# One-bank PSUM accumulators in the MLP, w1 loads spread over the last attention stage, layernorm transposes in the third step of a cycle

## The chip, the core and the metric

The kernel runs on one core of a Trainium2 chip. Five engines work side by side, each through its own list of instructions in order: TensorE (PE; its weight loads appear as PEld), VectorE (DVE), ScalarE (ACT), GpSimd (POOL) and SyncE (SP), which here only issues transfers. They wait for each other through semaphores. Matmul results go to PSUM, 8 banks of 128 partitions x 2 KB; a matmul of 512 float32 columns fills one bank. The metric is device time in microseconds; lower is better. The span in a trace reaches from the first to the last instruction.

## The reference

A transformer block on 2048 tokens of width 1024, all in bfloat16: attention with 32 heads of 32 and a causal window of 256 tokens, then an MLP of width 3584, each behind a layernorm without parameters and with a residual.

```python
def _A_ref(x, wqkv, wo):
    H = 32; Dh = D // H; W = 256
    qkv = (x @ wqkv).reshape(B, S, 3, H, Dh).transpose(2, 0, 3, 1, 4)
    q, k, v = qkv[0], qkv[1], qkv[2]
    scores = einsum("bhqd,bhkd->bhqk", q, k) * (Dh ** -0.5)
    mask = (idx[:, None] - idx[None, :] >= 0) & (idx[:, None] - idx[None, :] < W)
    p = softmax(where(mask, scores, -1e9))
    o = einsum("bhqk,bhkd->bhqd", p, v)
    return o.transpose(0, 2, 1, 3).reshape(B, S, D) @ wo
def _B_ref(x, w1, w2):
    return einsum("bsf,fd->bsd", silu(einsum("bsd,df->bsf", x, w1)), w2)
h  = A_x + _A_ref(layernorm(A_x), A_wqkv, A_wo)
h2 = h + _B_ref(layernorm(h), B_w1, B_w2)
```

## The kernel before

The 2048 tokens are worked in four blocks of 512 (`b`), each of four tiles of 128 (`j`). The order of the instructions is the order in which the code is written; nothing reorders it. Each engine takes its instructions in that order, and SP's transfers are issued in that order too.

The stages follow each other:

1. *Projection of block 0*: for each of four tiles a layernorm (`ln_stats`, `ln_rstd`, `ln_norm`), its transposes on PE and the v projection; then 16 groups for q and k (`qk_group`), with the layernorm of block 1 between them.
2. *Three attention stages* (`b` = 1, 2, 3): attention of block b-1, mixed with the projections of block b. A stage has 24 steps `n`, three for each of eight groups of four heads. A step computes the scores of one of three kinds of key pieces, `A`, `B`, `C` (PE), their exponentials (ACT) and masks (POOL), one projection group of eight matmuls (`dense[n]`, DVE casts it out), one piece of the tail of the head group before (`pending`), and perhaps one step of the next block's layernorm (`steps`). The tail has three pieces: in the first and second step of a cycle `attn_out` (attention times v into the tile `o_ps`, reciprocal and product on DVE), in the third `attn_transpose` (four transposes into the tile `tp_ps`, a DVE copy out).
3. *The last attention stage*: attention of block 3, where the 24 projection groups are the output projections of blocks 0 to 2 (`wo_group`). DVE adds the residual, a tile of `t_in` that SP loads (`load_res`), and the sum goes to `h_dram`. From step 9 on it also does the layernorm of block 0 for the MLP (`ln2_steps`), which begins with a load of h from `h_dram` (L316).
4. *The MLP*, block after block: 28 groups of the first product (`h1_group`, L402), each followed by `silu`, a tanh on ACT (L411) and a product on DVE (L412) that both read the accumulator; then eight groups of 28 matmuls of the second product (L444) with a residual add on DVE (L446) and a store, and the layernorm of the next block between them. The first block also takes in the rest of the attention tail and the output projection of block 3.

*Accumulators.* `next_acc` goes round the list `acc_banks`. Up to the MLP that is the two tiles `acc0` and `acc1` of one bank each. In the MLP four more banks join: the scores' tiles `sc0` and `sc1`, two banks each, of which each half is one accumulator (L397). The framework puts a wait ahead of an instruction that touches a tile which others still read or write.

```python
sc = [ps.tile([P, 2, 512], F32, name=f"sc{i}") for i in range(2)]            # L81
tp_ps = ps.tile([P, 1024], BF16, name="tp_ps")                               # L83
acc_banks += [sc[i][:, j, :] for i in range(2) for j in range(2)]            # L397
```

*Transposes.* A layernorm tile takes eight PE transposes into `tp_ps` (L173), which they fill, and one DVE copy out (L174). `attn_transpose` uses the same tile (L282, L283). In attention stages 1 and 2 a layernorm step is taken from step 4 on in the first two steps of each cycle: four of statistics, one reciprocal root (`ln_rstd`, L159 to L165, four Newton iterations of three instructions), four normalizations and four transposes, the last in steps 18, 19, 21 and 22.

*Loads.* All transfers are issued by SP. The eight w1 loads (L363, 896 KB each) come at once after the third attention stage, ahead of the first residual loads of the last one. w2 comes in seven pieces of 1 MB: piece 0 in step 9 of the last stage just ahead of the h load, the others in the MLP. `t_in` and `t_out` lie in the region `r_t`, which also holds the transposed layernorm of the odd blocks.

Of the kernel before, what the change touches and what calls it, by code (L numbers as in the profile page):

```python
# [14 lines left out]
P = 128  # L15
# [21 lines left out]
def kernel(  # L37
# [43 lines left out]
    sc = [ps.tile([P, 2, 512], F32, name=f"sc{i}") for i in range(2)]  # L81
# [72 lines left out]
    def ln_rstd(st, rs, lo, hi):  # L154
        n = hi - lo
        var = small.tile([P, 4], F32, name="ln_var", tag="ln_var")
        t = small.tile([P, 4], F32, name="ln_t", tag="ln_t")
        va, ta, y = var[:, 0:n], t[:, 0:n], rs[:, lo:hi]
        nc.vector.tensor_scalar(out=va, in0=st[:, lo:hi, 1], scalar1=LN_EPS, scalar2=None, op0=ALU.add)  # L159
        nc.vector.tensor_scalar(out=y.bitcast(I32), in0=va.bitcast(I32), scalar1=1, scalar2=None, op0=ALU.logical_shift_right)  # L160
        nc.vector.tensor_scalar(out=y.bitcast(I32), in0=y.bitcast(I32), scalar1=-1, scalar2=0x5F3759DF, op0=ALU.mult, op1=ALU.add)
        for _ in range(4):
            nc.vector.scalar_tensor_tensor(out=ta, in0=y, scalar=-0.5, in1=va, op0=ALU.mult, op1=ALU.mult)
            nc.vector.tensor_tensor(out=ta, in0=ta, in1=y, op=ALU.mult)
            nc.vector.scalar_tensor_tensor(out=y, in0=ta, scalar=1.5, in1=y, op0=ALU.add, op1=ALU.mult)  # L165
# [136 lines left out]
    def ln1_steps(b):  # L302
# [6 lines left out]
        for j in range(4):  # L309
            steps.append(lambda j=j: ln_transpose(xs[j], lnT_b[b % 2], j, dve))  # L310
        return steps
# [14 lines left out]
    steps = ln1_steps(1)  # L326
# [9 lines left out]
    for b in range(1, NB):  # L336
        dense = [lambda j=j, c=c: v_group(b, j, c, dve) for j in range(4) for c in range(2)]
        dense += [lambda w=w, g=g: qk_group(b, w, g, dve) for g in range(G) for w in range(2)]
        if b + 1 < NB:
            for j in range(4):  # L340
                load_x(b + 1, j)
            steps = ln1_steps(b + 1)
        else:
            steps = []
# [3 lines left out]
        for g in range(G):  # L348
            for kind in KINDS:
# [4 lines left out]
                if steps and n >= 4 and n % 3 != 2:  # L354
                    steps.pop(0)()
                n += 1
            pending = tail_of(b - 1, g)
        while steps:
            steps.pop(0)()


    for kt in range(KT):
        nc.sync.dma_start(out=w1[:, kt, :], in_=w1_v[:, kt, :])  # L363
# [7 lines left out]
    n = 0  # L371
    for g in range(G):
        for kind in KINDS:
# [7 lines left out]
            if pending:  # L381
                pending.pop(0)()
            if n == 9:
                steps = ln2_steps(0)
                nc.sync.dma_start(out=w2[0], in_=w2_v[:, 0:4, :])
# [11 lines left out]
    acc_banks += [sc[i][:, j, :] for i in range(2) for j in range(2)]  # L397
# [18 lines left out]
    for b in range(NB):  # L416
# [4 lines left out]
        for ft in range(FT):  # L421
# [7 lines left out]
            if b == 0 and 6 <= ft < 14:  # L429
# [3 lines left out]
                wo_group(NB - 1, j, c)  # L433
        if b == 0:
            load_w2(6)
        steps = ln2_steps(b + 1) if b + 1 < NB else []
        load_res(b, 0, h_dram)
# [47 lines left out]
```

## Time and profile before

| | us |
|---|---|
| median of 3 runs | 846.25 (846.16 to 846.5) |
| the profiled execution, its own time | 846.29 |
| its span | 844.6 |
| PE busy | 724.2 |
| PE weight loads busy (beside PE) | 353.4 |
| DVE busy | 329.5 |
| ACT busy | 257.1 |
| POOL busy | 171.6 |

Mean granted TensorE clock: 0.98 of full speed. DMA is 16.9% busy with the kernel's own queue.

How to read it: a busy time is the sum of an engine's instructions over the span. Engines work at the same time, so the times don't add up; the engine with the largest share sets the pace only where it is not itself waiting. The view of waits gives the idle time of an engine ahead of an instruction, by what ended it. The timeline shows instructions in order of time, neighbours of one kind merged (x16 is 16 of them), with the idle time ahead of the first one and its releaser in brackets. A few matmul records are missing, so x15 can stand for 16.

### The profile page before, as it was taken

How to read it: one execution, taken by the hardware profiler on the slowest of the kernel's cores; microseconds unless marked ns; L12 is line 12 of the kernel's file. 1: busy time of each engine (PE TensorE's matmuls, PEld its weight loads, DVE VectorE, ACT ScalarE, POOL GpSimd, SP SyncE). 2: the span in 40 equal slices, each digit the busy share in tenths (PEclk: the TensorE clock that was granted, in tenths of full speed). 3: DMA queues.
4: the chain of work that ended last, by engine and by line, in shares of the span. 5: the costliest groups of instructions: out<-in, count | busy, mean ns of one | idle time of the engine just before them, and what ended most of it. 6: DMA issues, size and time to landing. Idle time of an engine off the chain costs nothing.

```text
span 844.6 us, 12753 instructions
## 1 busy us (share of the span) xinstructions
PE 724.2 (86%) x5265; PEld 353.4 (42%) x5358; DVE 329.5 (39%) x738; ACT 257.1 (30%) x325; POOL 171.6 (20%) x375
## 2 busy tenths in 40 slices
PE   6999999999992978888779877789887889878898
PEld 2445555555551544433334433334333334333443
DVE  7446756754440456433324223223232242232111
ACT  3226557667771655311200022200022200122100
POOL 1006556666761645200000000000000000000000
PEclk9999999999996989999999999999999999999999
DMA  9310010010008242541041000021100020100010
GB/s 318 130 50 2 2 51 2 2 43 11 2 19 356 101 163 89 177 153 45 1 134 41 19 31 1 1 75 32 44 0 1 0 81 32 38 0 1 6 44 26
DMA packets 28138, 49.06 MB, mean 58 GB/s; under 512 B 1968, under 2 KB 12208, under 8 KB 28080
## 3 DMA queue, kind: packets, MB, share of 16 engines
q1 hardware_dynamic: 28080, 48.24, 16.9%
q8 instruction: 42, 0.69, 0.3%
q14 instruction: 16, 0.13, 0.0%
HBM read 39.85 MB, written 8.39 MB: 57 GB/s over the span
## 4 chain that ended last, share of the span: by engine, by line
PE 77%; DVE 10%; DMA 8%; ACT 3%; issue 2%; SPq 0%; ACTq 0%; DVEq 0%
PE sc L402 15%; PE sc L444 13%; PE acc L201 12%; PE acc L444 8%; PE acc L402 7%; PE acc L193 7%; PE acc L211 4%; PE o_ps L265 4%; PE sc L229 3%; DMA r_t<-in_A_x_dram 3%; DVE r_a L412 3%; DMA r_e<-h_dram 2%; ACT r_a L411 2%; DVE r_t L446 2%; PE tp_ps L173 1%
## 5 line engine op out<-in xcount | busy, mean ns | idle before, releaser
L240 ACT ACTIVATE r_e<-sc 128x1024 bf16<-128x1024 f32 (+2 forms) x192 | 175.8, 967 | 112.7 <-PE sc L229 112.7
L255 POOL TENSOR_SCALAR_AFFINE_SELECT r_e<-r_e 128x256 bf16<-128x256 bf16 (+1 forms) x368 | 168.6, 487 | 176.4 <-ACT r_e L240 172.5
L402 PEld LDWEIGHTS <-r_w 128*128 128x128 bf16 x896 | 87.1, 97 | 166.3 <-issue 65.0
L402 PE MATMUL sc<-r_e,r_w 128*128 128x512 bf16 x452 | 105.0, 379 | 41.4 <-DVE r_a L412 38.8
L444 PEld LDWEIGHTS <-r_a 128*128 128x128 bf16 x896 | 88.1, 99 | 121.9 <-issue 20.5
L444 PE MATMUL sc<-r_a 128*128 128x512 bf16 x548 | 125.9, 386 | 13.9 <-DVE r_t L446 13.3
L411 ACT ACTIVATE r_n<-sc 128x512 f32<-128x512 f32 x30 | 17.9, 597 | 252.4 <-PE sc L402 249.7
L444 PE MATMUL acc<-r_a 128*128 128x512 bf16 x327 | 73.7, 379 | 1.0 <-DMA r_a<-in_B_w_dram 0.6
L201 PEld LDWEIGHTS <-r_w 128*128 128x128 bf16 x512 | 46.1, 98 | 59.4 <-issue 10.3
L203 DVE CAST r_a<-acc 128x512 bf16<-128x512 f32 x56 | 38.5, 688 | 69.9 <-PE acc L201 69.7
L265 PE MATMUL o_ps<-r_a,r_e 128*128 128x33 bf16 x1440 | 46.4, 178 | 18.6 <-DVE r_n L273 18.6
L201 PE MATMUL acc<-r_t,r_w 128*128 128x512 bf16 x240 | 58.0, 380 | 3.0 <-issue 1.7
L265 PEld LDWEIGHTS <-r_e 128*128 128x128 bf16 x1440 | 45.9, 96 | 34.3 <-issue 19.7
L201 PE MATMUL acc<-r_w 128*128 128x512 bf16 x244 | 57.0, 379 | 1.7 <-issue 0.9
L211 PE MATMUL acc<-r_o,r_a 128*128 128x512 bf16 x195 | 51.5, 404 | 5.9 <-DVE r_t L213 4.3
L412 DVE SCALAR_TENSOR_TENSOR r_a<-r_n,sc 128x512 bf16<-128x512 f32 x30 | 20.6, 688 | 78.3 <-ACT r_n L411 78.3
L402 PE MATMUL acc<-r_e,r_w 128*128 128x512 bf16 x208 | 48.6, 379 | 0.4
L402 PE MATMUL sc<-r_a,r_w 128*128 128x512 bf16 x139 | 33.4, 378 | 13.7 <-DVE r_a L412 8.6
L446 DVE SCALAR_TENSOR_TENSOR r_t<-sc,r_t 128x512 bf16<-128x512 f32 x20 | 13.7, 684 | 77.1 <-PE sc L444 77.1
L229 PE MATMUL sc<-r_a 32*128 32x128 bf16 (+2 forms) x704 | 40.5, 279 | 0.0
L211 PEld LDWEIGHTS <-r_a 128*128 128x128 bf16 x256 | 24.0, 101 | 36.9 <-issue 14.2
L213 DVE TENSOR_TENSOR r_t<-acc,r_t 128x512 bf16<-128x512 f32 x26 | 17.8, 685 | 45.1 <-PE acc L211 25.3
(69 smaller groups left out, 509.7 us busy)
## 6 DMA issues: line engine op xcount, KB each, us to landing
r_w<-in_B_w_dram SPq DMA_DIRECT2D x8, 896.0 KB, 11.9
r_a<-in_B_w_dram SPq DMA_DIRECT2D x7, 1024.0 KB, 9.5
r_w<-in_A_wqkv_dram SPq DMA_DIRECT2D x6, 1024.0 KB, 11.2
r_o<-in_A_x_dram SPq DMA_DIRECT2D x16, 256.0 KB, 7.7
r_t<-in_A_x_dram SPq DMA_DIRECT2D x16, 256.0 KB, 2.8
h_dram<-r_t SPq DMA_DIRECT2D x16, 256.0 KB, 2.0
r_t<-h_dram SPq DMA_DIRECT2D x16, 256.0 KB, 2.8
out_dram<-r_t SPq DMA_DIRECT2D x32, 128.0 KB, 1.7
```

The lines of the kernel that those rows point to most:

```text
L193: nc.tensor.matmul(acc, lhsT=lnT_b[b % 2][:, kt, j * P:(j + 1) * P], rhs=wqkv[:, kt, col0:col0 + 512], start=(kt == 0), stop=(kt == KT - 1))
L201: nc.tensor.matmul(acc, lhsT=wqkv[:, kt, col0:col0 + P], rhs=lnT_b[b % 2][:, kt, :], start=(kt == 0), stop=(kt == KT - 1))
L203: copy(out=(qT, kT)[which][b][:, g, :], in_=acc)
L211: nc.tensor.matmul(acc, lhsT=qT[b][:, g, j * P:(j + 1) * P], rhs=wo[:, g, c * 512:(c + 1) * 512], start=(g == 0), stop=(g == G - 1))
L229: nc.tensor.matmul(sc[hh // 2][:, hh % 2, ch * P:(ch + nq) * P], lhsT=kT[t // 4][r0:r0 + DH, g, (t % 4) * P:(t % 4 + 1) * P], rhs=qT[b][r0 ...
L240: nc.scalar.activation(out=e[:, :, lo:hi], in_=sc[pair][:, :, lo:hi], func=ACT.Exp, scale=scale)
L255: nc.gpsimd.affine_select(out=ap, in_=ap, pattern=[[0, 2], [0, n], [sgn, P]], compare_op=ALU.is_ge if upper else ALU.is_gt, fill=0.0, base ...
L265: nc.tensor.matmul(o_ps[:, qt * 2 + hh, 0:VW], lhsT=e_of(i, kind, pair)[:, hh, ch * P:(ch + 1) * P], rhs=v[:, b * 4 + kt, g * 4 + pair * 2 ...
L402: nc.tensor.matmul(acc, lhsT=w1[:, kt, ft * P:(ft + 1) * P], rhs=ln2T[b][:, kt, :], start=(kt == 0), stop=(kt == KT - 1))
L411: nc.scalar.activation(out=th, in_=acc, func=ACT.Tanh, scale=0.5)
L412: nc.vector.scalar_tensor_tensor(out=gT[:, ft, :], in0=th, scalar=1.0, in1=acc, op0=ALU.add, op1=ALU.mult)
L444: nc.tensor.matmul(acc, lhsT=gT[:, ft, j * P:(j + 1) * P], rhs=w2[ft // 4][:, ft % 4, c * 512:(c + 1) * 512], start=(ft == 0), stop=(ft == ...
```

## The change

Five edits, in the order of the program.

- The scores' tiles `sc0`, `sc1` move to a pool of their own, which is closed ahead of the MLP. A new pool takes its place with four tiles of one bank each, `hacc0` to `hacc3`, and these join `acc_banks`.
- `ln_rstd` does three Newton iterations, not four.
- In attention stages 1 and 2 the layernorm steps start at step 1 (step 3 is left out), nine of them up to step 10; the four transposes are a list of their own, `turns`, taken in steps 11, 14, 17 and 20, the third steps of their cycles. The layernorm of block 1 keeps its order.
- The w1 loads are issued one by one in the even steps 0 to 14 of the last stage; w2's piece 0 moves from step 9 to step 17.
- In the MLP the first residual load of a block (`load_res(b, 0, h_dram)`) is issued ahead of w2's last piece.

```diff
@@ -78,7 +78,9 @@
-    sc = [ps.tile([P, 2, 512], F32, name=f"sc{i}") for i in range(2)]
+    ps_sc = tc.tile_pool(name="ps_sc", bufs=1, space=bass.MemoryType.PSUM, reuse_waits="tile")
+    sc_pool = ps_sc.__enter__()
+    sc = [sc_pool.tile([P, 2, 512], F32, name=f"sc{i}") for i in range(2)]
@@ -159,7 +161,7 @@
-        for _ in range(4):
+        for _ in range(3):
@@ -306,9 +308,7 @@
-        for j in range(4):
-            steps.append(lambda j=j: ln_transpose(xs[j], lnT_b[b % 2], j, dve))
-        return steps
+        return steps, [lambda j=j: ln_transpose(xs[j], lnT_b[b % 2], j, dve) for j in range(4)]
@@ -323,7 +323,7 @@
-    steps = ln1_steps(1)
+    steps = sum(ln1_steps(1), [])
@@ -339,9 +339,9 @@
-            steps = ln1_steps(b + 1)
+            steps, turns = ln1_steps(b + 1)
         else:
-            steps = []
+            steps, turns = [], []
@@ -351,16 +351,15 @@
-                if steps and n >= 4 and n % 3 != 2:
+                if steps and n >= 1 and n != 3:
                     steps.pop(0)()
+                elif turns and n % 3 == 2:
+                    turns.pop(0)()
                 n += 1
             pending = tail_of(b - 1, g)
-        while steps:
-            steps.pop(0)()
-
-
-    for kt in range(KT):
-        nc.sync.dma_start(out=w1[:, kt, :], in_=w1_v[:, kt, :])
+        assert not steps and not turns
@@ -380,8 +379,11 @@
+            if n % 2 == 0 and n // 2 < KT:
+                nc.sync.dma_start(out=w1[:, n // 2, :], in_=w1_v[:, n // 2, :])
             if n == 9:
                 steps = ln2_steps(0)
+            if n == 17:
                 nc.sync.dma_start(out=w2[0], in_=w2_v[:, 0:4, :])
@@ -394,7 +396,9 @@
-    acc_banks += [sc[i][:, j, :] for i in range(2) for j in range(2)]
+    ps_sc.__exit__(None, None, None)
+    ps_h1 = ctx.enter_context(tc.tile_pool(name="ps_h1", bufs=1, space=bass.MemoryType.PSUM, reuse_waits="tile"))
+    acc_banks += [ps_h1.tile([P, 512], F32, name=f"hacc{i}")[:] for i in range(4)]
@@ -431,10 +435,10 @@
+        load_res(b, 0, h_dram)
         if b == 0:
             load_w2(6)
         steps = ln2_steps(b + 1) if b + 1 < NB else []
-        load_res(b, 0, h_dram)
```

The line numbers of the changed kernel are others: L402 becomes L406, L444 becomes L448, L206 L208, L216 L218, L363 L383, L173 L175, L174 L176, L203 L205, L282 to L283 L284 to L285.

*PE in the first MLP product*, where one group ends and the next begins in the same two-bank tile; `sc_78` is `sc0`, `r_w` holds w1, `r_a` the transposed layernorm of block 0. Before:

```order
L402 MATMUL sc_78<-r_a,r_w 128x512
L402 LDWEIGHTS r_w
L402 MATMUL sc_78<-r_a,r_w 128x512 [waits DVE_49]
L402 LDWEIGHTS r_w
L402 MATMUL sc_78<-r_a,r_w 128x512
```

and at the same place now:

```order
L406 MATMUL hacc_4649<-r_a,r_w 128x512
L406 LDWEIGHTS r_w
L406 MATMUL hacc_4650<-r_a,r_w 128x512 [waits DVE_49]
L406 LDWEIGHTS r_w
L406 MATMUL hacc_4650<-r_a,r_w 128x512
```

The two groups write two tiles now, and each group has a wait of its own for DVE, also those on `acc` and on the first halves, which had none.

*DVE in attention stage 1*, around the first layernorm transpose. L203 casts a projection group out, L272 and L273 belong to `attn_out`, L283 copies the attention transposes out of `tp_ps`, L174 a layernorm tile. Before:

```order
L203 CAST r_a<-acc_82 128x512 [waits PE_49]
L283 COPY r_a<-tp_ps 128x512 [waits PE_49,Activation_49]
L203 CAST r_a<-acc_83 128x512 [waits PE_49]
L272 RECIPROCAL recip<-o_ps 128x8 [waits PE_49]
L273 TENSOR_TENSOR r_n<-o_ps,recip 128x4x64 [waits DVE_49]
L174 COPY r_w<-tp_ps 128x8x128 [waits PE_49]
```

and around the first one now:

```order
L205 CAST r_a<-acc_86 128x512 [waits PE_49]
L285 COPY r_a<-tp_ps 128x512 [waits PE_49,Activation_49]
L176 COPY r_w<-tp_ps 128x8x128 [waits PE_49]
L205 CAST r_a<-acc_85 128x512 [waits PE_49]
L274 RECIPROCAL recip<-o_ps 128x8 [waits PE_49]
L275 TENSOR_TENSOR r_n<-o_ps,recip 128x4x64 [waits DVE_49]
```

The layernorm copy has moved from behind `attn_out` to directly behind the copy of the attention transposes.

*SP at the begin of the last attention stage.* `r_w<-in_B_w_dram` is a w1 load, `r_t<-in_A_x_dram` a residual load, `h_dram<-r_t` a store of h; waits on DMAHW are for earlier transfers. Before, with six more w1 loads ahead:

```order
L363 DMA r_w<-in_B_w_dram 128x3584 [waits DMAHW6_49,PE_49]
L363 DMA r_w<-in_B_w_dram 128x3584 [waits DMAHW7_49]
L206 DMA r_t<-in_A_x_dram 128x1024 [waits DMAHW0_49,DVE_49]
L206 DMA r_t<-in_A_x_dram 128x1024 [waits DMAHW1_49]
L216 DMA h_dram<-r_t 128x1024 [waits DMAHW2_49,DVE_49]
L206 DMA r_t<-in_A_x_dram 128x1024 [waits DMAHW3_49,DMAHW0_49]
```

and now:

```order
L346 DMA r_o<-in_A_wo_dram 128x4x1024 [waits DMAHW7_49,DVE_49,PE_49]
L208 DMA r_t<-in_A_x_dram 128x1024 [waits DMAHW0_49,DVE_49,PE_49]
L208 DMA r_t<-in_A_x_dram 128x1024 [waits DMAHW1_49,PE_49]
L383 DMA r_w<-in_B_w_dram 128x3584 [waits DMAHW2_49]
L218 DMA h_dram<-r_t 128x1024 [waits DMAHW3_49,DVE_49]
L208 DMA r_t<-in_A_x_dram 128x1024 [waits DMAHW4_49,DMAHW0_49]
L383 DMA r_w<-in_B_w_dram 128x3584 [waits DMAHW5_49]
```

The residual loads stand ahead of w1 now, and one w1 load stands behind each further one.

## Rows read from the trace of the kernel before

**Rows 1.** The page: engines' busy us (share) xinstructions; granted clock in 40 slices.

```profile
PE 724.2 (86%) x5265; PEld 353.4 (42%) x5358; DVE 329.5 (39%) x738; ACT 257.1 (30%) x325; POOL 171.6 (20%) x375
...
PEclk9999999999996989999999999999999999999999
```

**Rows 2.** Waits of PE: engine line waited for, us in total, times, longest us.

```profile
PE sc L402 <- DVE r_a L412: 47.4, 33, 1.5
PE o_ps L265 <- DVE r_n L273: 18.6, 2, 16.6
PE sc L444 <- DVE r_t L446: 13.3, 8, 3.2
...
PE sc L402 <- DVE r_t L213: 4.9, 6, 1.0
...
PE acc L211 <- DVE r_t L213: 4.3, 1, 4.3
...
PE sc L402 <- DVE r_t L446: 2.4, 3, 0.8
```

**Rows 3.** Timeline, first MLP product of block 1: start us, us, engine, line.

```profile
498.57 0.69 DVE L412 SCALAR_TENSOR_TENSOR r_a<-r_a,sc 128x512 bf16<-128x512 f32 x1 [1.04 <-ACT r_a L411]
499.31 3.61 PE L402 MATMUL sc<-r_e,r_w 128*128 128x512 bf16 x16 [1.41 <-DVE r_a L412]
...
504.39 1.89 PE L402 MATMUL sc<-r_e,r_w 128*128 128x512 bf16 x8 [1.47 <-DVE r_a L412]
...
512.86 3.61 PE L402 MATMUL sc<-r_e,r_w 128*128 128x512 bf16 x16 [1.41 <-DVE r_a L412]
```

**Rows 4.** Timeline, PE: q and k groups of block 0; second MLP product.

```profile
29.52 17.43 PE L201 MATMUL acc<-r_w 128*128 128x512 bf16 x79
...
563.82 13.93 PE L444 MATMUL sc<-r_a 128*128 128x512 bf16 x55 [3.07 <-DVE r_t L446]
...
685.74 12.25 PE L444 MATMUL sc<-r_a 128*128 128x512 bf16 x55 [3.11 <-DVE r_t L446]
```

**Rows 5.** Timeline, PE: cycle starts ahead of the last attention stage; stops in it.

```profile
236.51 0.51 PE L229 MATMUL sc<-r_a 32*128 32x384 bf16 x8
...
244.53 0.51 PE L229 MATMUL sc<-r_a 32*128 32x384 bf16 x8
...
274.26 0.85 PE L265 MATMUL o_ps<-r_a,r_e 128*128 128x33 bf16 x24 [16.62 <-DVE r_n L273]
...
310.21 0.59 PE L211 MATMUL acc<-r_o,r_a 128*128 128x512 bf16 x1 [4.26 <-DVE r_t L213]
...
324.14 0.75 PE L265 MATMUL o_ps<-r_a,r_e 128*128 128x33 bf16 x24 [1.95 <-DVE r_n L273]
...
338.15 0.61 PE L173 MATMUL tp_ps<-ident,r_a 128*128 128x128 bf16 x8 [0.89 <-DVE r_a L283]
...
347.40 1.89 PE L402 MATMUL acc<-r_a,r_w 128*128 128x512 bf16 x8
```

**Rows 6.** Timeline, SP and DVE: the first residual loads of the last stage.

```profile
256.97 2.46 SPq L206 DMA_DIRECT2D r_t<-in_A_x_dram  x2
...
272.95 0.69 DVE L213 TENSOR_TENSOR r_t<-acc,r_t 128x512 bf16<-128x512 f32 x1 [19.50 <-DMA r_t<-in_A_x_dram]
```

**Rows 7.** DMA issues: transfers xcount, KB each, median us to landing.

```profile
r_t<-in_A_x_dram SPq DMA_DIRECT2D x16, 256.0 KB, 2.8
...
r_e<-h_dram SPq DMA_DIRECT2D x3, 1024.0 KB, 5.8
...
r_a<-h_dram SPq DMA_DIRECT2D x1, 1024.0 KB, 9.2
```

**Rows 8.** PE behind the root in stages 1, 2; one root instruction: us, mean ns.

```profile
93.11 1.89 PE L201 MATMUL acc<-r_t,r_w 128*128 128x512 bf16 x7 [1.00 <-DVE r_a L203]
...
157.74 1.89 PE L201 MATMUL acc<-r_w 128*128 128x512 bf16 x7 [0.47 <-DVE r_a L203]
...
L163 DVE SCALAR_TENSOR_TENSOR ln_t<-rs_a,ln_var 128x1 f32<-128x1 f32 x16 | 2.5, 159 | 0.6
```

## The prediction

> **What bounds the kernel now.** I read the busy times first, then what TensorE (PE) waited for, then PE's timeline stage by stage. PE is busy 724.2 us of a span of 844.6, all other engines 39% or less [rows 1], so the kernel is as long as PE's work plus PE's idle time: 120.4 us idle. The view of waits [rows 2] shows where it is: 47.4 + 4.9 + 2.4 = 54.7 us in the first MLP product (L402), 13.3 in the second (L444), 18.6 and 4.3 in attention and output projection. Six rows hold 90.9 of the 120.4.
>
> The MLP waits have one shape. In block 1 the DVE row at 498.57 is the silu's second half reading an accumulator until 499.26, and PE, idle for 1.41 us, starts at 499.31; the same follows at 504.39, and the pattern comes back at 512.86 [rows 3]. PE waits only on groups that write `sc`, never on `acc`. `sc0` and `sc1` are tiles of two banks with one accumulator in each half: the write of the second half waits until DVE has read the first half, which PE finished a moment before. A period of six groups takes 512.86 - 499.31 = 13.55 us. Without a stop, 80 matmuls of this shape (79 have a record) took 17.43 us with two one-bank tiles in turn [rows 4]: 0.2157 each when the last one's drain of some 0.17 is left out, so six groups of eight should take 10.35. Two stalls cost 3.20, or 1.60 each against 1.44 idle: 0.16 more than the view of waits says, for filling the array again.
>
> The second place is the last attention stage. It begins one cycle of three steps after 244.53, at 252.54, and ends at 347.40 where the MLP starts [rows 5]: 94.9 us for 24 steps. In the steady stage a cycle of three steps takes 244.53 - 236.51 = 8.02 us [rows 5], so 24 steps are 64.2. In between PE stands still for 16.62 us, from a residual load that was issued at 256.97 behind eight w1 loads and reached DVE at 272.95 [rows 6], then for 4.26 and 1.95 [rows 5], and the granted clock dips in just these slices (the 6 and the 8 in the page's clock row, [rows 1]).
>
> **The change, part by part.**
>
> *One-bank tiles.* Nothing is added to PE's work; each group now waits for the DVE read of its own bank, six groups earlier. Six groups are 10.35 us, and from the end of a group to DVE's release are some 1.5 us (the 1.41 above), so the wait is met long before. In the second product six groups are 6 x 28 x 0.2157 = 36 us. All of the 54.7 + 13.3 = 68.0 us in 33 + 6 + 3 + 8 = 50 stalls goes, and with each 0.16 us of refilling: 8.0. One more item is a clock that fell behind the stall at 563.82: the 56 matmuls behind it took 13.93 us where the same run at 685.74 took 12.25 [rows 4]; this 1.7 goes with its stall. What is late next there? DVE is: its residual add still stands behind statistics that wait for a load, but PE no longer stands behind DVE. I take **-78** of 77.7. The lower bound is 68.0, the idle alone; the upper is 80, if another run was slowed like that one. A satisfied wait on every group costs nothing that I can see: each of the ten groups in the 17.43 us run had one.
>
> The Trainium skill (Perfetto Trace Analysis, Optimizing Tensor Performance, Matmuls) asks that independent groups rotate through different PSUM banks, so that the evacuation of one overlaps the next one's matmuls. The kernel before does that already, through six, so by that sentence this part would bring nothing and the sum would be 830; rows 3 disagree, since the wait goes by tile and not by bank. It is rival D below.
>
> *w1 spread, w2 later.* The eight w1 loads leave the head of SP's queue; one is issued on every other step of the last stage. Past them move the two residual loads at its start. The first needs part of `lnT` in the last projection group to be read, so it goes out a little before the stage begins, lands after 2.8 us as loads of its size do [rows 7], and is there when DVE first wants it, some 2.4 us into the stage. The 16.62 us go. Every second step SP now has a store, a residual load and 896 KB of w1. These 1.4 MB fit in the 5.3 us of two steps: between the stage's begin and 272.95 [rows 6], 20.4 us, 7.4 MB of w1 and residual came in, 0.36 MB a microsecond, so they need some 4. And each residual load is issued ahead of its w1 piece and used two or three steps later. The load of h for the MLP's first layernorm (L316) no longer has w2 ahead of it: it took 9.2 us, the three later ones 5.8 [rows 7]. I take 5.8, as the w1 piece stands behind it on the queue. That ends the wait of DVE 3.4 us earlier, and PE's 4.26 us become about 0.9. The later stall of 1.95 comes from the chain of the reciprocal root on DVE, which has 12 instructions instead of 15 and frees about 0.6 to 0.8 of it, but DVE now comes to it with its statistics less cleared away; I take both places together at 3.0 us. The stage should be 64.2 + four layernorm transposes (2.2, at the 0.61 of such a row [rows 5] less its drain) + the one that meets the attention transpose, 0.89 [rows 5] + 0.16 + 3.0 + 0.5 for refilling = 71.0, against 94.9: **-23.9**. Bounds: none of these stalls but the 0.89 remains, -27.4; the h load lands as late as now, with its stalls and a clock that falls again, -17.
>
> *Transposes in the third step of each cycle.* This part I cost against the change. In that step PE runs the four attention transposes into `tp_ps` and, right behind them now, eight layernorm transposes into the same bank. DVE copies the bank out only after the cast of that step's projection. The last attention stage has one such meeting already: PE idle for 0.89 us at 338.15 [rows 5]; the other three transposes there, in other steps, have no wait. In stages 1 and 2 none has one now, and all four of each will: 8 x (0.89 + 0.16) = **+8.4**. The work of the transposes themselves is the same. PE sets the pace of these steps, so a step with fewer matmuls offers no cover. The lower bound is 0, if the copy is done in time, the upper +12, if DVE comes to the copy half a microsecond later in these stages than there.
>
> *Statistics and the root earlier.* The root's chain comes in step 6 instead of 10. It holds back DVE's next cast, and PE's stalls of 1.00 and 0.47 behind it [rows 8] go, but in the new place the attention transpose two steps later needs a result that queues behind the chain. With 12 instructions of 0.2 to 0.3 us that is 0 to 1.1 us in each of the two stages. I take **0** net, with 2 us either way. In the first layernorm PE waits for DVE itself, and one iteration less is three instructions of 159 ns plus gaps [rows 8]: **-0.6**, once, as PE is the slower one from the second tile on. The residual load ahead of the last w2 piece moves a transfer of 256 KB that waits for nothing: 0.
>
> The sum goes against the profiled execution, 846.29 us, 1.7 over its span; the median of the runs is 846.25. 846.3 - 78 - 23.9 + 8.4 + 0 - 0.6 = **752.2**, forecast 752.
>
> **Rivals.** *B: the transposes cost nothing*, because the third step leaves DVE and the bank free in time. For it: that step has the fewest PE instructions. Against it: the 0.89 us row, which is just this meeting. Time 752.2 - 8.4 = 744.
>
> *C: w1 collides in the last stage.* The pieces share the queues with the h load and the residual loads; the h load lands after 9 us or more, and the 4.26 and 1.95 us stalls stay, with the slow clock behind them. For it: the residual load at 256.97 shows how long a small load sits behind big ones. Against it: the pieces go out singly, and the small loads before them. The stage loses up to 6.9 of its 23.9, and residual loads that come late might add 2: 759 to 761.
>
> *D: the MLP stalls belong to neighbouring banks and not to the tile*, that is, to DVE reading one bank as PE writes the next, or the new tiles are still released together. Then only the other parts count: 846.3 - 23.9 + 8.4 - 0.6 = 830. Against it: `acc` groups next to each other never waited, and in the program each new tile has a wait of its own.
>
> *E, the slower side: the clock.* Without its pauses PE works through the MLP's 415 us in one go. If the granted clock went to its lower level (1.2 GHz) a matmul would take about twice 0.2157 us. The kernel would end later than before once 94 / 0.2157 = 436 of the MLP's some 1,860 matmuls ran so; if a third did, at 752 + 134 = 886. For it: only that such a stretch is not in the trace. Against it: the runs of 17.43 and 12.25 us without a pause at the full rate [rows 4], and that the clock's dips in the trace stand behind idle time.
>
> **How the numbers follow.** Forecast 0.73, with a range of its own from 748 to 758 (MLP 76 to 79, last stage 20 to 26, transposes 6 to 9, root 2 either way, not all at one end). B 0.10, C 0.13, D 0.02, E 0.02. The range of 8 in 10 takes in B's time and C's: **744 to 762**. Faster by over 0.2% (about what a measurement of this kernel can tell from no change): A to D, 0.98. E ends slower in most of its cases: 0.015, within 0.2% 0.005.
>
> **What would show it.** Right: in the waits of PE no row of L406 or L448 behind DVE's silu or residual add of any size; an MLP block of 101 us from the first product's start to the next block's; the last stage near 71 us with its first two residual loads landing within 3 us; eight idle times near 0.9 us of the layernorm transposes behind the copy at L285. Wrong: waits that stay on `hacc`, a clock below full in the MLP, a DVE wait over 3 us for h in the last stage, or transposes without a wait.

## The result and the profile after

The changed kernel takes 749.03 us in the median (747.96 to 749.97), the kernel before 846.2 beside it: a ratio of 0.8852, with an interval of 0.8837 to 0.8868. A second comparison gave 749.35 and 0.8871 (0.8851 to 0.8891). The forecast was 752, its range 744 to 762.

The profiled execution took 748.3 us with a span of 746.6. Its page, against [rows 1] (engines' busy us, share and instructions; granted clock in 40 slices):

```profile
span 746.6 us, 12719 instructions
...
PE 708.6 (95%) x5266; PEld 351.5 (47%) x5358; DVE 322.7 (43%) x705; ACT 257.1 (34%) x325; POOL 172.2 (23%) x375
...
PEclk9999999999999999999999999999999999999999
```

PE is idle for 38.0 us where it was idle for 120.4. The 6 and the 8 in the clock row are gone. The waits of PE after, against [rows 2] (engine, line waited for, us in total, times, longest us):

```profile
PE tp_ps L175 <- DVE r_a L285: 8.0, 9, 0.9
PE tp_ps L175 <- DVE r_e L176: 5.6, 6, 0.9
PE acc L195 <- ACT r_w L176: 4.5, 4, 1.1
...
PE o_ps L267 <- DVE r_n L275: 2.6, 2, 1.6
...
PE acc L213 <- DVE r_t L215: 0.2, 1, 0.2
```

No wait of L406 or L448 on DVE is left; the six rows that held 90.9 us have become 2.6 and 0.2. The longest row had one wait before, the 0.89 us at 338.15 [rows 5], and has nine now: layernorm transposes that wait for the copy of the attention transposes (L285).

The first MLP product of block 1, against [rows 3] (timeline of PE: start us, us, engine, line, operation):

```profile
463.64 7.07 PE L406 MATMUL hacc<-r_e,r_w 128*128 128x512 bf16 x32
...
474.00 7.07 PE L406 MATMUL hacc<-r_e,r_w 128*128 128x512 bf16 x32
```

Six groups take 474.00 - 463.64 = 10.36 us without a stop, where they took 13.55.

The last attention stage, against [rows 5]: its first scores, its four waits for DVE, and the first MLP matmul.

```profile
258.06 0.51 PE L231 MATMUL sc<-r_a 32*128 32x384 bf16 x8
...
293.58 1.89 PE L213 MATMUL acc<-r_o,r_a 128*128 128x512 bf16 x7 [0.18 <-DVE r_t L215]
296.51 0.77 PE L267 MATMUL o_ps<-r_a,r_e 128*128 128x33 bf16 x24 [1.04 <-DVE r_n L275]
...
306.31 0.75 PE L267 MATMUL o_ps<-r_a,r_e 128*128 128x33 bf16 x24 [1.61 <-DVE r_n L275]
...
318.81 0.61 PE L175 MATMUL tp_ps<-ident,r_a 128*128 128x128 bf16 x8 [0.89 <-DVE r_a L285]
...
328.05 1.89 PE L406 MATMUL acc<-r_a,r_w 128*128 128x512 bf16 x8
```

Stage 1 of the attention begins with this row before, and with this one after:

```profile
60.12 0.34 PE L229 MATMUL sc<-r_a 32*128 32x384 bf16 x4
```

```profile
59.68 0.34 PE L231 MATMUL sc<-r_a 32*128 32x384 bf16 x4
```

With these starts the span falls into four parts, each from one start to the next:

| us | before | after | change | predicted |
|---|---|---|---|---|
| up to attention stage 1 | 60.12 | 59.68 | -0.44 | -0.6 |
| attention stages 1 to 3 | 192.42 | 198.38 | +5.96 | +8.4 and 0 |
| last attention stage | 94.86 | 69.99 | -24.87 | -23.9 |
| MLP | 497.2 | 418.55 | -78.65 | -78 |
| span | 844.6 | 746.6 | -98.0 | -94.1 |

### The profile page after: what moved, and what is told of

Its sections match the earlier page's. It is cut to its first block, busy times and chain, and to the rows that moved or that the text cites. A ratio compares the mean times of both kernels' runs of the same rounds, so it can differ in the third digit from the quotient of the medians.

```text
span 746.6 us, 12719 instructions
## 1 busy us (share of the span) xinstructions
PE 708.6 (95%) x5266; PEld 351.5 (47%) x5358; DVE 322.7 (43%) x705; ACT 257.1 (34%) x325; POOL 172.2 (23%) x375
## 4 chain that ended last, share of the span: by engine, by line
PE 90%; DVE 5%; DMA 2%; issue 2%; ACT 1%; POOL 1%; DVEq 0%; ACTq 0%; POOLq 0%
PE hacc L406 17%; PE hacc L448 16%; PE acc L203 15%; PE acc L448 9%; PE acc L406 9%; PE acc L195 8%; PE o_ps L267 4%; PE acc L213 4%; PE sc L231 4%; PE tp_ps L175 2%; PE hacc L213 1%; DVE ln_st L153 1%; DMA r_a<-in_B_w_dram 1%; DMA r_a<-h_dram 1%; DVE r_t L450 1%
## 5 line engine op out<-in xcount | busy, mean ns | idle before, releaser
L448 PEld LDWEIGHTS <-r_a 128*128 128x128 bf16 x896 | 87.4, 98 | 105.0 <-issue 0.8
L406 PEld LDWEIGHTS <-r_w 128*128 128x128 bf16 x896 | 87.4, 98 | 104.8
L448 PE MATMUL hacc<-r_a 128*128 128x512 bf16 x548 | 121.4, 379 | 0.6
L406 PE MATMUL hacc<-r_e,r_w 128*128 128x512 bf16 x452 | 100.7, 379 | 0.3
L415 ACT ACTIVATE r_n<-hacc 128x512 f32<-128x512 f32 x30 | 17.9, 597 | 191.5 <-PE hacc L406 190.4
L205 DVE CAST r_a<-acc 128x512 bf16<-128x512 f32 x56 | 38.6, 690 | 83.6 <-PE acc L203 83.6
L448 PE MATMUL acc<-r_a 128*128 128x512 bf16 x327 | 73.7, 379 | 1.0 <-DMA r_a<-in_B_w_dram 0.5
L203 PEld LDWEIGHTS <-r_w 128*128 128x128 bf16 x512 | 46.0, 98 | 57.9 <-issue 8.9
L203 PE MATMUL acc<-r_t,r_w 128*128 128x512 bf16 x240 | 57.7, 380 | 2.2 <-issue 2.1
L203 PE MATMUL acc<-r_w 128*128 128x512 bf16 x245 | 56.7, 380 | 1.4 <-issue 1.3
L406 PE MATMUL acc<-r_e,r_w 128*128 128x512 bf16 x208 | 48.7, 379 | 0.4
L213 PE MATMUL acc<-r_o,r_a 128*128 128x512 bf16 x195 | 47.5, 380 | 1.6 <-issue 1.1
L450 DVE SCALAR_TENSOR_TENSOR r_t<-hacc,r_t 128x512 bf16<-128x512 f32 x20 | 13.7, 684 | 61.4 <-PE hacc L448 50.7
L213 PEld LDWEIGHTS <-r_a 128*128 128x128 bf16 x256 | 23.1, 98 | 29.8 <-issue 5.2
L416 DVE SCALAR_TENSOR_TENSOR r_a<-r_n,hacc 128x512 bf16<-128x512 f32 x30 | 20.6, 688 | 33.0 <-ACT r_n L415 33.0
L450 DVE SCALAR_TENSOR_TENSOR r_t<-acc,r_t 128x512 bf16<-128x512 f32 x12 | 8.3, 691 | 59.7 <-PE acc L448 59.7
L195 PE MATMUL acc<-r_w 128*128 128x512 bf16 x122 | 29.0, 380 | 5.1 <-ACT r_w L176 4.5
```

The source lines that it names most:

```text
L195: nc.tensor.matmul(acc, lhsT=lnT_b[b % 2][:, kt, j * P:(j + 1) * P], rhs=wqkv[:, kt, col0:col0 + 512], start=(kt == 0), stop=(kt == KT - 1))
L203: nc.tensor.matmul(acc, lhsT=wqkv[:, kt, col0:col0 + P], rhs=lnT_b[b % 2][:, kt, :], start=(kt == 0), stop=(kt == KT - 1))
L205: copy(out=(qT, kT)[which][b][:, g, :], in_=acc)
L213: nc.tensor.matmul(acc, lhsT=qT[b][:, g, j * P:(j + 1) * P], rhs=wo[:, g, c * 512:(c + 1) * 512], start=(g == 0), stop=(g == G - 1))
L406: nc.tensor.matmul(acc, lhsT=w1[:, kt, ft * P:(ft + 1) * P], rhs=ln2T[b][:, kt, :], start=(kt == 0), stop=(kt == KT - 1))
L416: nc.vector.scalar_tensor_tensor(out=gT[:, ft, :], in0=th, scalar=1.0, in1=acc, op0=ALU.add, op1=ALU.mult)
```

## The experiments

Each diff is against the changed kernel, where nothing else is said. In the comparisons of this section the kernel before, run beside the others, measured 844.7 to 846.0 in the median.

**The same kernel once more**, for what two executions of one program differ by.

> The changed kernel once more, beside the other three. Its four times lay between 747.96 and 749.97 with clocks of 1.000 to 0.997. Theory (the granted clock falls behind its stalls of 1.04 and 1.61 us in some executions and not in others): again two groups some 1.5 to 2 us apart, the longer ones with the lower clock. Rival (other causes): times spread evenly, without the clock.

Measured: 749.35 us in the median; the four times are 748.6, 748.89, 749.82 and 751.79, with mean granted clocks of 1.000, 0.999, 0.998 and 0.995. A longer time goes with a lower clock, as the theory has it, but two groups are not to be seen. Differences under 1 us between two kernels are therefore read from traces below, and not from medians. A trace is of one execution, so a stretch at the lower clock in it has to be looked for first.

**The tiles undone, and the tiles alone.**

```diff
# two-bank tiles again
...
-    sc = [sc_pool.tile([P, 2, 512], F32, name=f"sc{i}") for i in range(2)]
+    sc = [ps.tile([P, 2, 512], F32, name=f"sc{i}") for i in range(2)]
...
-    acc_banks += [ps_h1.tile([P, 512], F32, name=f"hacc{i}")[:] for i in range(4)]
+    acc_banks += [sc[i][:, j, :] for i in range(2) for j in range(2)]
```

The second kernel is the kernel before with only the opposite edit.

> The changed kernel with the scores' two-bank tiles as MLP accumulators again; all else as changed. Theory (the wait goes by tile): some 50 waits of PE behind the silu and the residual add come back, 68 us idle and 78 us in all, 749 + 78 = 827, with the last attention stage still near 70 us. Rival (the stalls belonged to neighbouring banks, or went for another reason): within 5 us of 749.

> The kernel before with the one-bank tiles alone. Theory: it loses just the MLP's waits, 846.2 - 78 = 768, the last attention stage stays at 95 us and the three stages ahead of it where they were. If the parts help each other the time is off 768 by more than 3 us; rival (neighbouring banks): 846.

Measured: 828.29 us and 767.55 us, one run each. The waits of PE with the two-bank tiles put back:

```profile
PE sc L402 <- DVE r_a L412: 47.4, 33, 1.5
PE sc L444 <- DVE r_t L446: 12.7, 8, 3.0
```

They are the rows of before [rows 2], with 12.7 for 13.3. With the tiles alone none of them is there, and the two of the last attention stage stay:

```profile
PE o_ps L267 <- DVE r_n L275: 18.2, 2, 16.5
...
PE acc L213 <- DVE r_t L215: 4.2, 1, 4.2
```

All four kernels use the same eight banks; what differs is whether two of them are one tile. So the MLP's part belongs to the tile, and it does not lean on the other edits. In the MLP itself it is 78.7 us with the tiles alone (497.20 - 418.54) and 78.3 when they are undone (496.85 - 418.55). The spans differ by a little more (844.6 - 765.7 = 78.9 and 826.6 - 746.6 = 80.0), since the stages ahead of the MLP ran at other clocks in these executions (table below). The kernel with the tiles alone doesn't have the fifth edit either, the residual load ahead of w2's last piece, and its MLP is as long as the changed kernel's: that edit is worth nothing, as forecast.

**w1 at once again, and w2's first piece early again.**

```diff
# w1 at once
+    for kt in range(KT):
+        nc.sync.dma_start(out=w1[:, kt, :], in_=w1_v[:, kt, :])
     dense = []
...
-            if n % 2 == 0 and n // 2 < KT:
-                nc.sync.dma_start(out=w1[:, n // 2, :], in_=w1_v[:, n // 2, :])
# the other kernel: w2[0] early
-            if n == 17:
+            if n == 9:
                 nc.sync.dma_start(out=w2[0], in_=w2_v[:, 0:4, :])
```

> The changed kernel with all eight w1 loads ahead of the last stage's residual loads again; w2's first piece stays at step 17. Theory: the first residual load lands some 16 us after its issue, PE stands still for 16 to 17 us once and its first matmuls after that run at the lower clock level (2 us more): 749 + 18 = 767. The h load stays near 5.6 us. Rival (the spread loads cost as much in little waits as they save): 755 to 760.

> The changed kernel with w2's first piece ahead of the h load again, at step 9. Theory: the h load lands after 9 us in place of 5.6, DVE's statistics wait 3.5 us longer, PE's stall of 0.18 behind them becomes 3 to 4, perhaps with a stretch at the lower clock level: 752.5 to 756. Rival (the w1 pieces, not w2's, set the landing): 749 to 750.

Measured: 767.03 us (one run), and 752.02 us (751.85 to 753.62). Timeline of PE with w1 at once, the one long wait of the stage:

```profile
279.65 0.85 PE L267 MATMUL o_ps<-r_a,r_e 128*128 128x33 bf16 x24 [16.47 <-DVE r_n L275]
```

It is the 16.62 of [rows 5]. With w2's piece ahead of the h load, that load takes 9.1 us (5.6 in the changed kernel), and PE stands still at its first use:

```profile
298.85 2.93 PE L213 MATMUL acc<-r_o,r_a 128*128 128x512 bf16 x7 [4.09 <-DVE r_t L215]
```

The load's row in the DMA issues (transfers, KB each, median us to landing):

```profile
r_a<-h_dram SPq DMA_DIRECT2D x1, 1024.0 KB, 9.1
```

That is the 4.26 of [rows 5], and the eight matmuls behind it (seven have a record) take 2.93 us where such a row takes 1.90. Behind this idle time the clock has fallen towards its lower level of 1.2 GHz (granted 0.61 from 298.85 to 302), as it had in the kernel before (0.50 from 310.2 to 314.9). The stage lasts 73.96 us (259.42 to 333.38) where the changed kernel's lasts 69.99. So both moves of loads are needed. The first is worth 18.9 us of the stage (88.90, from 258.08 to 346.98, against 69.99), of which the one wait is 16.5. The second is worth 4.0 in the stage of the profiled execution, the longest of its four, and 3.0 by the medians.

**The layernorm transposes out of the third step.** Three kernels try it, with the edit in attention stages 1 and 2:

```diff
# (a) other steps
-                elif turns and n % 3 == 2:
+                elif turns and n % 3 != 2:
# (b) other steps, none ahead of the normalizations: 12, 13, 15, 16
-                elif turns and n % 3 == 2:
+                elif turns and not steps and n % 3 != 2:
# (c) the same third steps, but ahead of the step's projection group
                 scores(b - 1, g, kind)
+                if turns and not steps and n % 3 == 2:
+                    turns.pop(0)()
                 dense[n]()
```

> The changed kernel with the layernorm transposes of attention stages 1 and 2 in the first and second steps of the cycles (steps 12, 13, 15, 16), beside the attention product. Theory (the meeting in the transposes' tile costs): eight idle times of 0.89 us go, 749 - 7 = 742. Rival (those steps are heavier, so the transposes cost more there): 749 or more.

> The changed kernel with one edit: in attention stages 1 and 2 the four layernorm transposes are taken in steps 12, 13, 15 and 16, first and second steps of their cycles, all behind the normalizations. The theory of the meeting (a layernorm transpose waits for the copy of the attention transposes out of the same tile only where both stand in one step): the eight idle times of 0.89 us at the layernorm transposes of these stages go, 7.1 us in all, 742 us (741 to 744). The rival, that the transposes cost the same in any step because DVE is busy with casts there: 748 to 749.

> The changed kernel with the layernorm transposes still in the third steps, but ahead of the projection group and not behind the attention transposes. Theory: PE's work is the same as with the changed kernel and no meeting is left, 742, as with the transposes in other steps. Rival (the third step itself is the wrong place): 749.

In (a) two of the four transposes of a stage come in steps 0 and 3, and not in 12 to 16 as its expectation has it. That is ahead of the normalizations, so they turn tiles that are not yet normalized; the instructions are the same in number and size. (b) and (c) keep the order.

Measured: (a) 742.49 us (741.86 to 743.5), (b) 741.19 (740.78 to 742.8), (c) 742.22 (741.62 to 743.48). A meeting in the changed kernel, timeline of PE:

```profile
88.50 0.39 PE L284 MATMUL tp_ps<-ident,r_n 128*128 128x128 bf16 x4
89.77 0.61 PE L175 MATMUL tp_ps<-ident,r_o 128*128 128x128 bf16 x8 [0.89 <-DVE r_a L285]
```

and the same step in (c):

```profile
88.33 0.62 PE L175 MATMUL tp_ps<-ident,r_o 128*128 128x128 bf16 x8
89.00 1.67 PE L203 MATMUL acc<-r_t,r_w 128*128 128x512 bf16 x7
90.51 0.39 PE L284 MATMUL tp_ps<-ident,r_n 128*128 128x128 bf16 x4
90.83 0.34 PE L231 MATMUL sc<-r_a 32*128 32x384 bf16 x4
```

In (c) a projection group of eight matmuls stands between the two users of `tp_ps`, and DVE has copied the tile out by then. In the waits of (b) and (c) the row of L175 behind L285 has come down to the one of the last stage:

```profile
PE tp_ps L175 <- DVE r_a L285: 0.9, 1, 0.9
```

So it isn't the third step that costs; it is two users of one PSUM tile with nothing between them.

**Four Newton iterations again, and the old schedule of the layernorm.**

```diff
# the root as before
-        for _ in range(3):
+        for _ in range(4):
# the other kernel: the steps of stages 1 and 2 as before, root in step 10
-            steps, turns = ln1_steps(b + 1)
+            steps, turns = sum(ln1_steps(b + 1), []), []
...
-                if steps and n >= 1 and n != 3:
+                if steps and n >= 4 and n % 3 != 2:
                     steps.pop(0)()
-                elif turns and n % 3 == 2:
-                    turns.pop(0)()
```

> The changed kernel with four Newton iterations. Theory: PE's first layernorm wait is 0.4 to 0.5 us longer, the stall of 1.61 us in the last stage grows by 0.6 to 0.9, and the stages 1 and 2 get a stall of up to 0.5 each: 750 to 752. Rival (DVE has slack for it everywhere but at the start): 749.5.

> The changed kernel with the layernorm steps of attention stages 1 and 2 put back where the kernel before has them: from step 4 on, first and second steps of a cycle alone, root in step 10, transposes in steps 18, 19, 21 and 22. All else as changed, three Newton iterations among it. Meetings gone: -7.1 us. The root comes back in step 10: with 12 instructions in place of 15 I expect one or two idle times of PE of 0.2 to 0.7 us behind it (the kernel before has 1.00 and 0.47). 742.5 us (741.5 to 744). If the earlier root is worth 1.5 us, this kernel is that much above the one with the transposes in steps 12 to 16; if it is worth nothing, the two are within 0.5 us and no idle time follows the root in step 10.

Measured: 754.07 us (752.4 to 755.25), and 741.54 (741.31 to 742.77). Timeline of PE with four iterations, root in step 6 as in the changed kernel, the new wait in stage 1 (stage 2 has one of 0.55 at 151.40):

```profile
83.75 0.40 PE L284 MATMUL tp_ps<-ident,r_n 128*128 128x128 bf16 x4 [0.63 <-DVE r_n L275]
```

With three iterations and the root in step 10, the only wait behind the root:

```profile
93.36 1.89 PE L203 MATMUL acc<-r_t,r_w 128*128 128x512 bf16 x8 [0.23 <-DVE r_a L205]
```

Three iterations in either step cost 0.23 us or nothing; four cost 1.18 in the one step and 1.47 in the other [rows 8]. That 754.07 is above the 750 to 752 I expected has two other causes in the profiled execution. In the last stage the fourth iteration makes the 1.61 of the changed kernel 2.72, the granted clock behind it is 0.88 (310.88 to 324.75), and the stage takes 72.63 us (261.37 to 334.00). And stage 1 begins 2.1 us later, of which 1.7 are a lower clock under the first matmuls of the v projection; kernels with three iterations show that too (last section), so it is not the iteration's doing.

**The last stage laid anew, and one transpose at a time in the MLP.** The second kernel is the first with one more edit.

```diff
# on top of (b)
+    LN2_AT = {8: 1, 10: 1, 11: 1, 12: 1, 13: 1, 15: 1, 16: 2, 17: 2, 18: 1, 19: 1, 21: 1, 22: 1}
...
-            if n == 9:
+            if n == 8:
                 steps = ln2_steps(0)
...
-            if steps and n >= 9:
+            for _ in range(LN2_AT.get(n, 0)):
                 steps.pop(0)()
# the second kernel, on top of that, in the second MLP product
                     nc.tensor.matmul(acc, lhsT=gT[:, ft, j * P:(j + 1) * P], ...
+                    if ft == 13 and j * 2 + c >= 5 and steps:
+                        steps.pop(0)()
...
-                for _ in range(2):
+                for _ in range(2 if j * 2 + c < 5 else 1):
```

> Transposes of stages 1 and 2 in steps 12, 13, 15 and 16 as in the kernel that only does that, and the layernorm of the last attention stage laid anew: h load in step 8 (not 9), statistics in steps 10 to 13, root in step 15 (not 14, so behind the evacuation of that step's attn_out and with two free steps ahead of the next one), normalizations two each in steps 16 and 17, transposes in 18, 19, 21 and 22 (first and second steps; not 20). In the changed kernel PE idles 0.18, 1.04, 1.61 and 0.89 us in this stage, 3.7 in all. Theory that each comes from what stands ahead on DVE or in the tile: at most 1 us of it remains, the stage takes 66 to 67 us where it takes 69.99, the whole 738 to 739. Rival, that DVE is overfull here and the delay only moves: the stage stays at 69 to 70, 741 to 742. If the granted clock's drop in this stage needs a stall of 1.6 us or more ahead of it, no such drop is seen here in any profile.

> As the kernel with the last stage laid anew, and in the second MLP product the layernorm transposes are taken one at a time (not two in a row) from group 5 on: one in the middle of a group of 28 matmuls, one at its end. In the changed kernel the second of two transposes in a row waits 0.93 us for the copy of the first out of the same tile, six times, 5.6 us in all. Theory: all six go, 5 to 5.6 us below the kernel without this edit, 732.5 to 734. Rival, that a transpose inside an accumulation group costs as much by a break in the run of matmuls (0.2 us or more each at twelve places): 736 to 738.

Measured: 737.21 us (736.98 to 739.23), and 730.35 (729.8 to 731.9), a ratio to the kernel before of 0.8646 (0.863 to 0.8662). In the first, one wait is left in the last stage:

```profile
288.27 0.77 PE L267 MATMUL o_ps<-r_a,r_e 128*128 128x33 bf16 x24 [0.49 <-DVE r_n L275]
```

The stage takes 66.58 us; in the second it has no wait at all and takes 66.16 (both from the table below). In the MLP, two transposes in a row in the changed kernel, and one at a time in the second kernel (timelines of PE):

```profile
428.59 0.61 PE L175 MATMUL tp_ps<-ident,r_e 128*128 128x128 bf16 x8
430.13 0.61 PE L175 MATMUL tp_ps<-ident,r_e 128*128 128x128 bf16 x8 [0.93 <-DVE r_e L176]
```

```profile
411.14 3.18 PE L449 MATMUL acc<-r_a 128*128 128x512 bf16 x14
414.17 0.61 PE L175 MATMUL tp_ps<-ident,r_e 128*128 128x128 bf16 x8
414.61 3.19 PE L449 MATMUL acc<-r_a 128*128 128x512 bf16 x14
```

In a row, the second starts 1.54 us after the first; alone, the next matmul starts 0.44 us after it. That is 1.10 each, 6.6 for six, and the MLP went from 418.4 to 411.77 us. The break in a group of matmuls costs nothing that shows. This is more than the 5 to 5.6 expected, since I had counted the idle column (0.93) and not the distance of the starts.

The starts of the stages in these traces, each the first row of its scores or of L406 (L402, L404 or L407 where the lines differ) in the timeline of PE:

| | stage 1 | last stage | MLP | stages 1 to 3 | last stage lasts |
|---|---|---|---|---|---|
| changed kernel | 59.68 | 258.06 | 328.05 | 198.38 | 69.99 |
| two-bank tiles again | 59.64 | 258.02 | 329.75 | 198.38 | 71.73 |
| kernel before, tiles alone | 61.52 | 253.94 | 347.16 | 192.42 | 93.22 |
| w1 at once | 59.70 | 258.08 | 346.98 | 198.38 | 88.90 |
| w2 early | 61.03 | 259.42 | 333.38 | 198.39 | 73.96 |
| four iterations | 61.78 | 261.37 | 334.00 | 199.59 | 72.63 |
| old schedule | 61.15 | 252.27 | 322.54 | 191.12 | 70.27 |
| (b) other steps | 59.34 | 250.32 | 320.90 | 190.98 | 70.58 |
| (c) ahead of the projection | 61.26 | 251.24 | 323.22 | 189.98 | 71.98 |
| last stage anew | 59.62 | 250.61 | 317.19 | 190.99 | 66.58 |
| and one at a time | 59.59 | 250.57 | 316.73 | 190.98 | 66.16 |

## Why the prediction was right, and where its terms were off

**One-bank tiles, -78: right, -78.65.** Rows as forecast: no wait of L406 or L448 on DVE, a block of 100.7 us (from the first product's start at 444.65 to the next block's at 545.31) where 101 was written, and the full clock in the MLP. That the stalls go by the tile was argued from [rows 3]; the two-bank tiles put back, and the one-bank tiles alone, show it, and rival D (830) falls. Here the Trainium skill (PSUM — Partial Sum Buffer, section PSUM bank collisions raise a hardware error) has the finer rule: guard PSUM by bank and quadrant, by bank in its simple version. The two halves of `sc` are two banks, so a wait by bank would not have held PE; 828.29 against 749.03 us is what the coarser guard by tile costs. In the changed kernel each of these tiles is one bank, so its waits are the simple version of the rule; what happens without a guard no run here shows.

**Loads in the last stage, -23.9: right, -24.87, and each load for its own share.** The first two residual loads go out ahead of w1, and h comes in 5.6 us (5.8 was taken). The two residual loads land after 3.7 us, where 2.8 was taken and 3 was the sign to look for; DVE does not wait for them. Timeline of SP, the row of the h load in the DMA issues, and DVE's wait for it:

```profile
256.64 0.82 SPq L208 DMA_DIRECT2D r_t<-in_A_x_dram  x2
257.51 1.51 SPq L383 DMA_DIRECT2D r_w<-in_B_w_dram  x1
```

```profile
r_a<-h_dram SPq DMA_DIRECT2D x1, 1024.0 KB, 5.6
```

```profile
291.44 1.29 DVE L153 BATCH_NORM_STATS2 ln_st<-r_a 128x6 f32<-128x512 bf16 x2 [2.92 <-DMA r_a<-h_dram]
```

The floor of the stage was put at 64.2 + 2.2 = 66.4 us; the kernel without any wait there takes 66.16. The rest was put at 0.89 + 0.16 + 3.0 + 0.5 = 4.55 and measured 3.83 (69.99 - 66.16), of which 3.72 are the four waits shown above. The 3.0 for two places came out as 0.18 + 1.04 + 1.61 = 2.83 in three. The 1.04, where DVE does the statistics of a tile from 293.78 on, ahead of the `attn_out` that PE waits for, is not named in the prediction, and the stall behind the h load is 0.18 and not 0.9; that the total is so near is in part luck. DVE itself waited 2.92 us for h, just under the 3 us that the prediction set as its bound. Rival C (759 to 761) falls: what it feared, an h load of 9 us, happens with w2's piece ahead of it, and costs 4 us of the stage there, 752.0 in all.

**Transposes in the third step, +8.4: mechanism and count right, size 1.0 too high.** Eight meetings were forecast and eight came, each with the 0.89 us of [rows 5]; rival B (744, no wait) falls. The step that was mis-sized is the 0.16 of refilling on each. It came from the MLP, where a stop is followed by another group of the same matmuls. At a meeting the two starts are 89.77 - 88.50 = 1.27 us apart; where a projection group or scores follow the attention transposes they are some 0.32 (90.83 - 90.51), so a meeting costs 0.95 and eight 7.6. By the stages, 198.38 - 190.98 = 7.40 with (b); (c) would give 8.40, but 1.0 of that has another source (end of the last section). The part was worth taking back: (b) and (c) beat the changed kernel by 7 us.

**Statistics and the root, 0 net: wrong by 1.4 us.** The prediction let the idle times of 1.00 and 0.47 [rows 8] go and put as much back in the new place, 0 to 1.1 us a stage for a chain of 12 instructions. The changed kernel has no wait behind the chain there. What counts is the chain's length and not its place: by the two kernels above, three iterations cost 0.23 us or nothing in either step, and the fourth 1.2 to 1.5: 199.59 against 198.38 in the early step, 192.42 (before) against 191.12 in the old one. Moving the root from step 10 to step 6 is worth 191.12 - 190.98 = 0.14, with the transposes in other steps of the same kind. So one iteration less was worth about 1.3 us in these stages, which the sum sets off against a cost that did not come; it was counted only in the start (-0.6, measured -0.44) and inside the last stage.

These are the 3.9 us by which the sum of the terms (-94.1) missed the spans (-98.0): 1.0 of refilling, 1.4 of the root, 1.0 in the last stage, 0.65 in the MLP, and 0.16 the other way at the start. All but the last were taken too dear.

**Rival E, the clock, falls.** Windows of the changed kernel: start and end, length, busy us (instructions) by engine, granted clock, DMA share, GB/s.

```profile
250.00:330.00 80.00, 74.55 (x937) 41.80 (x950) 45.09 (x106) 52.45 (x55) 51.32 (x111) 1.00 0.56 197
...
328.00:746.00 418.00, 406.66 (x1969) 188.48 (x2005) 142.91 (x255) 67.08 (x113) 1.35 (x4) 1.00 0.15 49
```

418 us with PE busy for 406.66 of them stay at the full clock, the level of 2.4 GHz; the prediction had judged this from runs of 12 to 17 us [rows 4]. Its 415 us for the MLP should have read 419 (497.2 - 78), which changes nothing in it.

## What to carry to other kernels

In this framework a wait goes by what the program calls a tile: two accumulators that are to be used in turn must be two tiles, even where they already lie in two banks. Two users of one PSUM tile, one behind the other in PE's list, cost a wait for the evacuation each time (0.95 and 1.10 us here); put work that PE has anyway between them, which took 7 us out of the attention stages and 6.6 out of the MLP here. Where a chain of small instructions sits in front of an engine's evacuations, ask how long it is before asking where it stands, and take what a wait costs from the distance of two starts, not from the idle column.

## What the runs showed of the hardware

**The clock at the start differs between executions.** The first 16 matmuls of the v projection, in the changed kernel and in (c), where the program up to there is the same (timelines of PE):

```profile
9.96 3.63 PE L195 MATMUL acc<-r_w 128*128 128x512 bf16 x16 [1.10 <-ACT r_w L176]
```

```profile
9.85 5.31 PE L195 MATMUL acc<-r_w 128*128 128x512 bf16 x16 [1.10 <-ACT r_w L176]
```

In the windows of (c) the granted clock is 0.91 over the first 20 us; the same window of the changed kernel has 1.00:

```profile
0.00:20.00 20.00, 15.43 (x60) 6.27 (x62) 15.01 (x62) 4.97 (x6) 2.96 (x7) 0.91 0.96 317
```

The granted clock of 0.91 is a mean: part of that stretch ran at the lower level of 1.2 GHz. PE had run the same instructions before it in both, the matmuls of L147 and the first tile's transposes. Of 14 profiled executions here, six have the slow row (5.07 to 5.31 us) and begin stage 1 at 61.03 to 61.78; eight have 3.63 us and begin it at 59.34 to 60.12. So these 1.4 to 1.7 us are most of what separates the starts near 61.2 from those near 59.6 in the table. That they also make much of the spread of the times of one kernel fits the granted clocks on record, but is not shown: one execution in each comparison has a trace.

**The same stall is followed by a slow clock in one execution and not in another.** Behind a wait of 1.95 us for L275 in the last stage, (c) ran at 0.89 and (b), with the same wait, at 1.00 (windows of (c), then of (b)):

```profile
299.00:314.00 15.00, 12.70 (x151) 6.83 (x153) 9.07 (x21) 7.75 (x8) 7.56 (x17) 0.89 0.56 177
```

```profile
298.00:312.00 14.00, 11.97 (x159) 6.92 (x159) 9.24 (x21) 7.75 (x8) 7.81 (x17) 1.00 0.60 190
```

In (c) part of the stretch is at 1.2 GHz. From that wait to the stage's last one it takes (c) 13.88 us and (b) 12.51, which is nearly all of the 1.4 us between their last stages. The length of the wait alone does not decide it. Ten profiled executions have a wait of 1.61 or 1.95 us for this product (L275, L273) in the last stage. From it to the stage's last wait seven of them take 12.50 or 12.51 us; three take 13.88 to 14.02: (c), the kernel before (1.95) and the kernel with the two-bank tiles again (1.61, with a granted clock of 0.88 from 306.4 to 320.5). The changed kernel, also with 1.61, has 1.00 there. What decides it stays open; the two kernels whose waits in the last stage are 0.49 us or none show no drop there in their profiles.

**A DVE instruction on four elements has no one duration.** The same instruction of the root in the changed kernel, in the last attention stage and in the MLP (timeline of DVE):

```profile
302.75 0.56 DVE L166 TENSOR_TENSOR ln_t<-ln_t,rs_b 128x4 f32<-128x4 f32 x1
...
414.22 0.16 DVE L166 TENSOR_TENSOR ln_t<-ln_t,rs_b 128x4 f32<-128x4 f32 x1
```

In the attention stages, where POOL masks at the same time (51.32 us of 80 in the window above), these instructions take 0.16 to 0.56 us; the MLP, with POOL idle, has 0.16 and 0.17. That POOL is the cause is argued and not shown: no run took the masks away.

**What (c) gains on.** (c) has its stages 1 to 3 1.0 us shorter than (b) (189.98 against 190.98), with no wait on DVE in either. It gains on the first scores of a cycle, in the eight cycles behind steps 11, 14, 17 and 20 of stages 1 and 2 (timelines of PE, (b) and then (c)):

```profile
88.47 0.46 PE L231 MATMUL sc<-r_a 32*128 32x384 bf16 x4
88.86 1.90 PE L203 MATMUL acc<-r_t,r_w 128*128 128x512 bf16 x8
```

```profile
90.83 0.34 PE L231 MATMUL sc<-r_a 32*128 32x384 bf16 x4
91.10 1.90 PE L203 MATMUL acc<-r_t,r_w 128*128 128x512 bf16 x8
```

From these scores to the projection group behind them it is 0.39 us in (b) and 0.27 in (c) in stage 1, and 0.44 and 0.33 in stage 2: some 0.9 us in all. Why they are shorter stays open.
